# Reordering the first attention steps and the first block of a fused attention, gated MLP and top-2 expert kernel

## The chip, the cores and the metric

One core of one Trainium2 chip runs the whole program. The metric is the device time of one execution in microseconds (us). Engines carry the names of the profile: PE is TensorE, DVE is VectorE, ACT is ScalarE, POOL is GpSimd, SP is SyncE, whose queue issues nearly all of the plain loads.

## The reference

Three parts follow one another: attention inside chunks of 64 positions, a gated MLP in float32 precision, and a mixture of 8 experts of which every token uses two.

```python
q, k, v: (4, 8, 576, 64)                       # batch, heads, positions, width of a head
scores = matmul(q_c, k_c.T) / sqrt(64)         # in chunks of 64 positions
attn = exp(scores - max); attn /= sum + 1e-9
x = matmul(attn, v_c)                          # 2304 tokens x 512
h = x @ w_in                                   # 512 x 2048
x = (h * clip(h + 3, 0, 6) / 6) @ w_out        # 2048 x 512
# then: noisy gate, top 2 of 8 experts, w * (relu(x @ w1[e]) @ w2[e]), summed
```

## The kernel before

The 2304 tokens are 18 tiles of 128, in five blocks of 4, 3, 4, 4 and 3 tiles. Each block runs through 16 **units** of the MLP; unit u holds 128 of the 2048 hidden columns. Precision comes from splitting each operand into a high part `hi` and a rest `lo`, and from three products per matmul (hi·hi, hi·lo, lo·hi: `PASSES`). In a unit, `mlp_s1` multiplies the block's tokens by w_in (12 matmuls of 128x512), `mlp_act` makes the activation g (ACT writes r at L329, DVE finishes r at L330, ACT writes g's hi part at L331), `mlp_lo` (DVE, L336) makes g's lo part, and `mlp_o` adds g times w_out to four accumulators (12 matmuls). PE works one unit ahead: `mlp_o` of unit u comes after `mlp_s1` of unit u+1.

In block 0 the weights aren't there yet in that form. They arrive as 32 **halves** of 512 KB in a 64-bit format: half 2u is w_in of unit u, half 2u+1 its w_out. Each half is turned into hi and lo by five steps: a shift (DVE, L162), the sign bits (DVE, L163), the low bits (DVE, L171), the hi part (ACT, `conv_hi`, L178) and the lo part (DVE, `conv_lo`, L185). The first two are `conv_1`, the third is `conv_2`, and each of the three DVE steps before the hi part reads what the one ahead of it wrote. Block 0 converts in unit u the halves b = 2u+3 and a = 2u+4. When the low bits of half s are done, half s+7 (for s < 10) or s+3 (for s >= 14) is loaded into the raw buffer that came free (`load64`, L150).

Attention of block 0's tiles 0 to 3 stands ahead of block 0, written out by hand, with the first conversions and with matmuls on a constant (`keep_warm`, L679) between. Attention of block 1's three tiles runs inside block 0, four units for each, as pieces k = 0 to 3: scores and row maximum and half of the exponentials (k = 0), the others, the sum's reciprocal and half of the scaling (k = 1), the rest of the scaling (k = 2), transposes and the product with v (k = 3). The functions `att_sc`, `att_mx`, `att_e`, `att_r`, `att_n`, `att_ns`, `att_pt`, `att_at`, `att_xo`, `att_hi`, `att_lo` are these pieces. PE's pieces are put between matmuls by `tick`.

On PE, DVE and ACT the order of the program is the order in which the Python code calls these functions (`manual_schedule`), and each engine works off its own list in that order, one instruction waiting for its inputs while all behind it wait too. SP's list is in program order as well.

Of the kernel before, what the change touches and what calls it, by code (L numbers as in the profile page):

```python
# [19 lines left out]
P = 128  # L20
# [32 lines left out]
def tile_kernel(ctx, tc, qkv, w1u, w2u, wg, noise, out):  # L53
# [89 lines left out]
    def load64(s):  # L143
        if 0 <= s < 2 * U1:
            if s in (3, 4, 5, 6, 10, 11, 12, 13):
                i = (s - 3) % 7
                raw = rawx[i // 2][:, (i % 2) * 2 * DM:(i % 2 + 1) * 2 * DM]
            else:
                raw = work.tile([P, 2 * DM], I32, tag="raw", bufs=3, name="raw")
            nc.sync.dma_start(raw, w1u[s // 2, s % 2])  # L150
            st["raw64", s] = raw

    def conv_1(s):
        if s >= 2 * U1:
            return
        j, h = divmod(s, 2)
        if h == 0:
            st["w", "m", j] = wpool.tile([P, 2, 2 * DM], F32R, tag="w", bufs=U1, name="w")
        raw = st["raw64", s].rearrange("p (n c) -> p n c", c=2)
        hi32 = raw[:, :, 1]  # L160
        u = work.tile([P, DM], I32, tag="x2", bufs=3, name="u")
        nc.vector.tensor_scalar(u, hi32, 3, 0x3fffffff, op0=ALU.logical_shift_left, op1=ALU.bitwise_and)  # L162
        nc.vector.scalar_tensor_tensor(u, hi32, -0x40000000, u, op0=ALU.bitwise_and, op1=ALU.bitwise_or)  # L163
        st["u", s] = u

    def conv_2(s):
# [5 lines left out]
        load64(s + 7 if s < 10 else s + 3 if s >= 14 else -1)  # L172

    def conv_hi(s):
        if s >= 2 * U1:
# [14 lines left out]
    def att_sc(t, pair=0):  # L190
        qt, kt, vt = st["qkv", t]
        sc = middle(pair).rearrange("p (r h k) -> p r h k", r=2, h=KD)
        for hp in range(KD):
            for c in range(2):
                for r in range(2):
                    s = slice(r * 64, r * 64 + 64)
                    nc.tensor.matmul(sc[c * 64:c * 64 + 64, r, hp, :], qt[s, hp, c, :], kt[s, c, hp, :],  # L197
                                     start=True, stop=True)
        st["sc", t] = sc
# [22 lines left out]
        else:  # L222
            nc.scalar.activation(sm, sm, AF.Exp, scale=0.125)

    def att_r(t):
# [3 lines left out]
        nc.vector.tensor_scalar(su, su, 1e-9, None, op0=ALU.add)  # L229
        nc.vector.reciprocal(su, su)  # L230

    def att_n(t):
        att_r(t)
        sm, su, mx, acts = st["att", t]
        nc.vector.tensor_tensor(sm, sm, su.to_broadcast([P, 8, 64]), op=ALU.mult)

    def att_ns(t, heads):
        sm, su, mx, acts = st["att", t]
# [11 lines left out]
    def att_at(t, at):  # L250
        nc.scalar.activation(at.rearrange("p k n -> p (k n)"), st.pop(("pt", t)), AF.Copy)
        st["attT", t] = at

    def att_xo(t, pair=0):
# [35 lines left out]
    def s1(dst, w, x, t0, n):  # L290
        k = 0
        for kd in range(KD):
            for a, b in PASSES:
                nc.tensor.matmul(dst, w[:, a, kd * P:(kd + 1) * P], x[:, b, kd, t0:t0 + n],  # L294
                                 start=(k == 0), stop=(k == 3 * KD - 1))
                k += 1
                if k % 4 == 0:
                    tick()

    def s2(acc, g, w, tiles, first, last):  # L300
        for i in range(tiles):
            gi = tile_of(g, i)
            for j, (a, b) in enumerate(PASSES):
                nc.tensor.matmul(acc[i][:gi.shape[2]], gi[:, a], w[:, b, DM:],  # L304
                                 start=(first and j == 0), stop=(last and j == 2))
            tick()
# [12 lines left out]
    def mlp_s1(b, u, g, off):  # L319
        n = BT[b] * P  # L320
        h = hbank(n)
        s1(h, st["w", "m", u], xb[b], 0, n)
        st["h", b] = h
        st["g", b, u] = g[:, off:off + 2 * n].rearrange("p (j n) -> p j n", j=2)

    def mlp_act(b, u):
# [4 lines left out]
        nc.scalar.activation(st["g", b, u][:, 0], r, AF.Copy)  # L331
        st["r", b] = r

    def mlp_lo(b, u):
        g = st["g", b, u]
# [409 lines left out]
    with tc.manual_schedule(engines={nc.tensor.engine, nc.vector.engine, nc.scalar.engine}):  # L745
        att_sc(0, 0), att_mx(0, False), att_e(0), att_n(0)
        keep_warm(7)
        att_sc(1, 1), att_pt(0, 0), att_at(0, at_[0])
        att_mx(1, True), att_e(1)
        att_sc(2, 2), att_mx(2, True)  # L750
        att_sc(3, 3), att_mx(3, False)
        att_xo(0, 0), att_hi(0), att_e(3), att_e(2)
        keep_warm(3)
        att_n(1), att_pt(1, 1), att_at(1, at_[1])
        keep_warm(5)
        att_lo(0), conv_1(0)
        att_n(3), att_pt(3, 3), att_xo(1, 1), att_hi(1), att_at(3, at_[0])
        att_n(2), att_pt(2, 2), att_at(2, at_[1])
        conv_2(0), conv_hi(0)
        att_lo(1)  # L760
        att_xo(3, 3), att_hi(3), att_xo(2, 2), att_hi(2)
        conv_lo(0), att_lo(3), att_lo(2)
# [98 lines left out]

    def block0():
        nonlocal prev
        n0 = st.get("tick", 0)
        for i in range(BT[1]):
            k = n0 + 28 * i
            t = LT + i
            at(ticks, k + 3, att_sc, t)
            at(ticks, k + 3 * 7 - 4 + 3, att_pt, t)
            at(ticks, k + 3 * 7 + 3, att_xo, t)  # L870
        for u in range(U1):

            t, k = LT + u // 4, (u % 4 if u < 4 * BT[1] else None)
# [11 lines left out]
            b, a = 2 * u + 3, 2 * u + 4  # L885
            conv_1(b)
            mlp_lo(0, u)
            conv_2(b)
            conv_hi(b)
            if k == 0:  # L890
                att_mx(t, True)
                att_e(t, range(4))
            elif k == 1:
                att_r(t)
                att_ns(t, range(4))
            elif k == 3:
                att_hi(t)
# [196 lines left out]
```

## Time and profile before

| | before |
|---|---|
| three runs, us | 935.14, 935.76, 937.75 (median 935.76) |
| the profiled execution, us | 934.58 |
| its span in the profile, us | 932.8 |
| PE / DVE / ACT busy over the span | 98% / 52% / 36% |
| PE's granted clock over the span | 0.998 of full |

The shares are averages over a span of which the part at issue is about an eighth: block 0 and the attention ahead of it end near 126 us, and there DVE is the busy engine.

### The profile page before, as it was taken

To read this page: it belongs to the slowest core of one execution; us is meant where nothing else is said; L and a number is where in the kernel's file an instruction comes from. 1 tells how busy PE (TensorE), PEld (TensorE's weight loads), DVE (VectorE), ACT (ScalarE), POOL (GpSimd) and SP (SyncE) were. 2 spreads that over 40 slices of the span, in tenths; PEclk is the share of its full clock that TensorE was granted. 3 is DMA by queue.
4 is the path that set the end of the run, shared out by engine and by line. 5 is a ranking of instruction groups with operands and counts; after the bars stand their busy time and mean duration, and the time that the engine had idled before them with its cause. 6 is when DMAs were issued, how large, how long until landed. Compare 5 with 4: busy or idle time off the path is not lost.

```text
span 932.8 us, 14436 instructions
## 1 busy us (share of the span) xinstructions
PE 913.1 (98%) x5814; PEld 766.3 (82%) x5814; DVE 482.2 (52%) x912; ACT 333.2 (36%) x643; POOL 231.9 (25%) x213
## 2 busy tenths in 40 slices
PE   6999999999999999999999999999999999999996
PEld 3677788887777777788988898898988889888885
DVE  6999965454454443537543555444545454441311
ACT  5565433333233322344541443333434333321210
POOL 0000000030002000033203345754645445332321
PEclk9999999999999999999999999999999999999999
DMA  9636639113112410024541764653746355240422
GB/s 342 204 112 193 193 98 372 61 37 101 35 34 58 136 35 1 1 69 113 156 139 15 191 145 116 151 121 113 145 117 128 111 128 127 69 54 20 54 25 33
DMA packets 49916, 101.49 MB, mean 109 GB/s; under 512 B 17040, under 2 KB 23056, under 8 KB 49840
## 3 DMA queue, kind: packets, MB, share of 16 engines
q1 hardware_dynamic: 38736, 80.38, 27.4%
q0 software_dynamic: 11104, 20.10, 11.9%
q8 instruction: 47, 0.77, 0.4%
q14 instruction: 29, 0.24, 0.1%
HBM read 77.66 MB, written 22.75 MB: 108 GB/s over the span
## 4 chain that ended last, share of the span: by engine, by line
PE 86%; DVE 10%; ACT 2%; issue 1%; DMA 0%; POOL 0%; POOLq 0%; DVEq 0%; ACTq 0%
PE bp L304 41%; PE bp L294 40%; DVE u L171 2%; DVE u L163 2%; DVE u L162 1%; DVE r L330 1%; DVE w L185 1%; DVE g L336 1%; PE pair L197 1%; PE pair L264 1%; PE pair L247 1%; ACT w L178 1%; PE bp L581 0%; ACT r L329 0%; DMA xr<-x2d,tab 0%
## 5 line engine op out<-in xcount | busy, mean ns | idle before, releaser
L304 PE MATMUL bp<-w,g 128*128 128x512 f32 (+1 forms) x1812 | 453.9, 396 | 0.4 <-ACT g L331 0.3
L304 PEld LDWEIGHTS bp<-w,g 128*128 128x128 f32 (+1 forms) x1812 | 328.3, 185 | 73.7 <-DVE g L336 0.8
L294 PE MATMUL bp<-Xa,w 128*128 128x304 f32 (+3 forms) x1344 | 244.2, 332 | 2.3 <-ACT w L178 1.9
L294 PEld LDWEIGHTS bp<-Xa,w 128*128 128x128 f32 x1344 | 209.0, 188 | 30.4 <-ACT w L178 5.2
L554 POOL DMA_INDIRECT xrq<-x2d,iq x114 | 119.5, 1048 | 95.7 <-DVE iq L548 34.4
L597 DVE SCALAR_TENSOR_TENSOR g<-bp,g 128x304 fp32r<-128x304 f32 (+2 forms) x128 | 60.4, 472 | 130.9 <-ACT g L596 130.9
L139 DVE TENSOR_TENSOR w<-raw,w 128x1024 fp32r<-128x1024 f32 x64 | 78.4, 1226 | 89.0 <-ACT w L138 89.0
L519 POOL DMA_INDIRECT table<-pay,slot x36 | 36.3, 1009 | 338.9 <-DVE slot L516 247.9
L596 ACT ACTIVATE g<-bp 128x304 fp32r<-128x304 f32 (+2 forms) x128 | 54.3, 424 | 168.6 <-PE bp L294 168.5
L294 PE MATMUL bp<-Xb,w 128*128 128x384 f32 (+1 forms) x480 | 106.1, 366 | 0.0
L294 PE MATMUL bp<-Xe,w 128*128 128x304 f32 (+1 forms) x672 | 102.7, 308 | 0.0
L294 PEld LDWEIGHTS bp<-Xe,w 128*128 128x128 f32 x672 | 99.8, 188 | 3.3
L330 DVE SCALAR_TENSOR_TENSOR r<-r,bp 128x512 f32<-128x512 f32 (+1 forms) x80 | 50.6, 632 | 91.8 <-ACT r L329 91.6
L294 PEld LDWEIGHTS bp<-Xb,w 128*128 128x128 f32 x480 | 85.3, 188 | 12.5 <-issue 1.8
L624 POOL DMA_INDIRECT out_dram<-arena,tab x40 | 62.7, 1567 | 123.5 <-DVE arena L621 100.1
L329 ACT ACTIVATE r<-bp,b 128x512 f32<-128x512 f32 (+1 forms) x80 | 51.3, 642 | 106.4 <-PE bp L294 106.4
L138 ACT ACTIVATE w<-raw 128x1024 fp32r<-128x1024 f32 x64 | 67.7, 1058 | 58.8 <-PE bp L304 58.5
L336 DVE TENSOR_TENSOR g<-r,g 128x512 fp32r<-128x512 f32 (+1 forms) x80 | 51.0, 637 | 40.2 <-ACT g L331 40.2
L331 ACT ACTIVATE g<-r 128x512 fp32r<-128x512 f32 (+1 forms) x80 | 47.2, 590 | 60.3 <-DVE r L330 60.3
L178 ACT ACTIVATE w<-u 128x512 fp32r<-128x512 f32 x32 | 20.3, 633 | 32.5 <-DVE u L171 32.5
L372 DVE STREAM_TRANSPOSE arena<-xrq 128x512 f32<-128x512 f32 (+1 forms) x30 | 31.4, 1046 | 0.1
L735 POOL MEMSET zero<- 128x1024 f32 x1 | 1.0, 952 | 115.1 <-DVE u L171 115.1
(148 smaller groups left out, 483.8 us busy)
## 6 DMA issues: line engine op xcount, KB each, us to landing
raw<-in_w2u_dram SPq DMA_DIRECT2D x64, 512.0 KB, 4.0
raw<-in_w1u_dram SPq DMA_DIRECT2D x24, 512.0 KB, 4.9
arena<-in_qkv_dram SPq DMA_DIRECT2D x14, 768.0 KB, 4.1
out_dram<-zero SPq DMA_DIRECT2D x4, 1536.0 KB, 19.4
rawx<-in_w1u_dram SPq DMA_DIRECT2D x8, 512.0 KB, 8.4
x2d<-x SPq DMA_DIRECT2D x15, 256.0 KB, 3.4
xq<-x2d SPq DMA_DIRECT2D x44, 64.0 KB, 3.4
xrq<-x2d,iq POOLq DMA_INDIRECT x114, 2.6
```

The costliest lines, as they stand in the source:

```text
L138: nc.scalar.activation(w[:, 0], raw, AF.Copy)
L139: nc.vector.tensor_tensor(w[:, 1], raw, w[:, 0].bitcast(F32), op=ALU.subtract)
L294: nc.tensor.matmul(dst, w[:, a, kd * P:(kd + 1) * P], x[:, b, kd, t0:t0 + n], start=(k == 0), stop=(k == 3 * KD - 1))
L304: nc.tensor.matmul(acc[i][:gi.shape[2]], gi[:, a], w[:, b, DM:], start=(first and j == 0), stop=(last and j == 2))
L329: nc.scalar.activation(r, st["h", b], AF.Relu, bias=b3)
L330: nc.vector.scalar_tensor_tensor(r, r, 6.0, st["h", b], op0=ALU.min, op1=ALU.mult)
L331: nc.scalar.activation(st["g", b, u][:, 0], r, AF.Copy)
L336: nc.vector.tensor_tensor(g[:, 1], st["r", b], g[:, 0].bitcast(F32), op=ALU.subtract)
L554: nc.gpsimd.indirect_dma_start(out=xr[:, c * P:(c + 1) * P], out_offset=None, in_=x2q, in_offset=bass.IndirectOffsetOnAxis(ap=st["iq", key ...
L596: nc.scalar.activation(g[:, 0, t0:t0 + n], h, AF.Relu)
L597: nc.vector.scalar_tensor_tensor(g[:, 1, t0:t0 + n], h, 0.0, g[:, 0, t0:t0 + n].bitcast(F32), op0=ALU.max, op1=ALU.subtract)
L624: s = nc.gpsimd.indirect_dma_start(out=out, out_offset=bass.IndirectOffsetOnAxis(ap=tab[:n, i, 0:1], axis=0), in_=y, in_offset=None, compu ...
```

## The change

It changes the order of the steps ahead of block 0 and in block 0, and nothing behind.

- The conversion is cut into `conv_1`, `conv_2`, `conv_3`, and the load that follows it is a call of its own, `load_next`.
- Ahead of block 0: halves 0 and 2 (w_in of units 0 and 1) are converted, of half 1 only two steps; tile 1's scaling goes to POOL, tile 0's copy of the transposes to DVE; the tiles use other PSUM pairs; 18 constant matmuls instead of 28; tiles 4 and 5 are loaded between the halves.
- In block 0: half a comes ahead of half b, the steps of both are interleaved with others, half b's lo part is made in the next unit (`late`), and attention starts two units later (`lag`).
- `mlp_s1` and `mlp_o` of block 0 take all of one product, then all of the next.

```diff
+    def load_next(*halves):
+        for s in halves:
+            load64(s + 7 if s < 10 else s + 3 if s >= 14 else -1)
...
+        passes = None
+        if b == 0:
+            passes = ((0, 0), (1, 0), (0, 1)) if u == 0 else ((0, 0), (0, 1), (1, 0))
+        s1(h, st["w", "m", u], xb[b], 0, n, passes)
...
-        att_sc(1, 1), att_pt(0, 0), att_at(0, at_[0])
+        att_sc(1, 3), att_pt(0, 0)
         att_mx(1, True), att_e(1)
...
-        keep_warm(6)
-        conv_1(1), conv_2(1), conv_hi(1)
-        conv_1(2), conv_2(2), conv_hi(2)
-        conv_lo(1), conv_lo(2)
+        att_at(0, at_[0], True)
+        att_sc(2, 1), att_mx(2, False), att_e(2)
+        att_sc(3, 2), att_mx(3, True), att_e(3)
+        att_xo(0, 0)
+        keep_warm(4, "p2")
+        att_r(1), att_nm(1, nc.gpsimd)
+        att_n(2), conv_1(0)
+        att_pt(1, 3), att_at(1, at_[1])
+        att_pt(2, 1), att_at(2, at_[0])
+        att_xo(1, 3), att_hi(0)
+        att_n(3), att_pt(3, 2)
+        conv_2(0), conv_3(0)
+        att_at(3, at_[1]), att_hi(1)
+        att_xo(2, 1), att_xo(3, 2)
+        conv_hi(0), att_hi(2), att_hi(3)
+        att_lo(0), att_lo(1), conv_lo(0), att_lo(2), att_lo(3)
+        conv_1(2), conv_2(2), conv_3(2), conv_hi(2)
+        conv_1(1), conv_2(1)
+        load_next(0)
...
             mlp_s1(0, u, gtile(), 0)
+            mlp_r(0, u)
             if k == 3:
                 att_at(t, at_[0])
-            mlp_act(0, u)
+            mlp_g(0, u)
+            if u == 0:
+                conv_3(1), conv_hi(1), conv_lo(2)
+                load_next(1, 2)
+                late = [1]
+            else:
+                conv_lo(*late)
...
-            conv_1(b)
-            mlp_lo(0, u)
-            conv_2(b)
-            conv_hi(b)
+            conv_1(a), conv_2(a)
+            mlp_lo(0, u)
+            if u == 0:
+                conv_lo(*late)
+            conv_1(b)
+            conv_3(a), conv_hi(a)
+            conv_2(b)
             if k == 0:
                 att_mx(t, True)
+            elif k == 1:
+                att_r(t)
+            elif k == 3:
+                att_hi(t)
+            conv_3(b), conv_hi(b)
+            conv_lo(a)
+            if k == 0:
                 att_e(t, range(4))
             elif k == 1:
-                att_r(t)
                 att_ns(t, range(4))
...
-            conv_1(a)
-            conv_2(a)
-            conv_hi(a)
-            conv_lo(b)
-            if k == 3:
-                att_lo(t)
-            conv_lo(a)
+            late = [b]
+            load_next(b, a)
```

DVE, block 0, from the finishing of r in one unit to the same step in the next, in a unit without attention on DVE. `u` with a number is the half being converted, `w` its split form, `r` and `g` the activation. Before (unit 2; L171 is the low bits, L185 the lo part):

```order
L330 SCALAR_TENSOR_TENSOR r_558<-r_558,bp4_428 128x512
L162 TENSOR_SCALAR u_578<-raw_354 128x512
L163 SCALAR_TENSOR_TENSOR u_578<-raw_354,u_578 128x512
L336 TENSOR_TENSOR g_545<-r_558,g_545 128x512
L171 SCALAR_TENSOR_TENSOR u_578<-raw_354,u_578 128x512
L162 TENSOR_SCALAR u_587<-raw_405 128x512
L163 SCALAR_TENSOR_TENSOR u_587<-raw_405,u_587 128x512
L171 SCALAR_TENSOR_TENSOR u_587<-raw_405,u_587 128x512
L185 TENSOR_TENSOR w_536<-u_578,w_536 128x512
L185 TENSOR_TENSOR w_586<-u_587,w_586 128x512
L330 SCALAR_TENSOR_TENSOR r_614<-r_614,bp3_427 128x512
```

And now (unit 1; the same steps are L352, L160, L167, L364, L174, L191):

```order
L352 SCALAR_TENSOR_TENSOR r_468<-r_468,bp3_411 128x512
L191 TENSOR_TENSOR w_391<-u_445,w_391 128x512
L160 TENSOR_SCALAR u_486<-rawx_120 128x512
L167 SCALAR_TENSOR_TENSOR u_486<-rawx_120,u_486 128x512
L364 TENSOR_TENSOR g_455<-r_468,g_455 128x512
L160 TENSOR_SCALAR u_490<-rawx_120 128x512
L174 SCALAR_TENSOR_TENSOR u_486<-rawx_120,u_486 128x512
L167 SCALAR_TENSOR_TENSOR u_490<-rawx_120,u_490 128x512
L174 SCALAR_TENSOR_TENSOR u_490<-rawx_120,u_490 128x512
L191 TENSOR_TENSOR w_485<-u_486,w_485 128x512
L352 SCALAR_TENSOR_TENSOR r_513<-r_513,bp4_412 128x512
```

Between the last low-bits step and the next r two lo parts stood before; now one stands there, and the other has moved behind r.

ACT, block 0, the unit that starts a tile's attention (k = 0), up to the next unit's r and g. Rows with `w<-u` are hi parts, rows with `mx` and x4 are four exponentials. Before (unit 0 and the start of unit 1):

```order
L329 ACTIVATE r_462<-bp4_428,b3_81 128x512
L331 ACTIVATE g_433<-r_462 128x512
L178 ACTIVATE w_408<-u_466 128x512
L220 ACTIVATE arena_94,su_475<-pair0_72,mx_473 128x64 x4
L178 ACTIVATE w_481<-u_482 128x512
L329 ACTIVATE r_503<-bp3_427,b3_81 128x512
```

And now (unit 2 and the start of unit 3):

```order
L351 ACTIVATE r_513<-bp4_412,b3_81 128x512
L356 ACTIVATE g_500<-r_513 128x512
L184 ACTIVATE w_546<-u_547 128x512
L184 ACTIVATE w_485<-u_551 128x512
L226 ACTIVATE arena_94,su_558<-pair0_72,mx_556 128x64 x4
L351 ACTIVATE r_584<-bp3_411,b3_81 128x512
```

The exponentials stood between the two hi parts and stand now between the second hi part and the next unit's r.

## Rows read from the trace of the kernel before

**Rows 1.** Busy time by stretch: us, then each engine's busy us, granted PE clock, DMA share, GB/s.

```profile
10.00:20.00 10.00, 6.36 (x150) 4.17 (x148) 8.45 (x21) 7.64 (x38) 0.00 (x0) 1.00 1.03 408
24.26:123.92 99.66, 97.27 (x576) 72.56 (x577) 94.50 (x169) 54.80 (x141) 0.95 (x1) 1.00 0.51 160
```

**Rows 2.** Timeline of DVE, unit 12 of block 0: start us, us, engine, line.

```profile
106.47 0.68 DVE L330 SCALAR_TENSOR_TENSOR r<-r,bp 128x512 f32<-128x512 f32 x1
...
107.52 0.69 DVE L163 SCALAR_TENSOR_TENSOR u<-raw,u 128x512 int32<-128x512 int32 x1
...
109.34 0.42 DVE L162 TENSOR_SCALAR u<-raw 128x512 int32<-128x512 int32 x1
109.79 0.69 DVE L163 SCALAR_TENSOR_TENSOR u<-raw,u 128x512 int32<-128x512 int32 x1
110.52 0.69 DVE L171 SCALAR_TENSOR_TENSOR u<-raw,u 128x512 int32<-128x512 int32 x1
111.13 1.47 DVE L185 TENSOR_TENSOR w<-u,w 128x512 fp32r<-128x512 f32 x2
112.52 0.68 DVE L330 SCALAR_TENSOR_TENSOR r<-r,bp 128x512 f32<-128x512 f32 x1
```

**Rows 3.** Timeline of ACT beside the end of that unit.

```profile
111.24 0.63 ACT L178 ACTIVATE w<-u 128x512 fp32r<-128x512 f32 x1 [1.16 <-DVE u L171]
111.78 0.67 ACT L329 ACTIVATE r<-bp,b 128x512 f32<-128x512 f32 x1
113.23 0.63 ACT L331 ACTIVATE g<-r 128x512 fp32r<-128x512 f32 x1 [0.78 <-DVE r L330]
```

**Rows 4.** Timeline of ACT, units 0 and 1: exponentials (first and fourth) and scalings.

```profile
31.94 0.32 ACT L220 ACTIVATE arena<-pair,mx 128x64 f32<-128x64 f32 x1 [0.23 <-DVE mx L209]
...
32.83 0.32 ACT L220 ACTIVATE arena<-pair,mx 128x64 f32<-128x64 f32 x1
...
38.45 1.05 ACT L240 ACTIVATE arena<-arena,su 128x64 f32<-128x64 f32 x4
```

**Rows 5.** Timeline of DVE, unit 0: the row maximum and its scaling.

```profile
30.96 0.68 DVE L205 TENSOR_REDUCE mx<-pair 128x8 f32<-128x512 f32 x1
31.68 0.17 DVE L209 TENSOR_SCALAR mx<-mx 128x8 f32<-128x8 f32 x1
```

**Rows 6.** DMA issues of the page: count, KB each, median us to landing.

```profile
raw<-in_w2u_dram SPq DMA_DIRECT2D x64, 512.0 KB, 4.0
raw<-in_w1u_dram SPq DMA_DIRECT2D x24, 512.0 KB, 4.9
```

**Rows 7.** Timeline, units 6 and 7: half 18 is issued, half 18 is used.

```profile
70.35 2.12 SPq L150 DMA_DIRECT2D raw<-in_w1u_dram  x2
...
76.75 0.42 DVE L162 TENSOR_SCALAR u<-raw 128x512 int32<-128x512 int32 x1
```

**Rows 8.** Timeline of the steps ahead of block 0 and of its first r.

```profile
10.06 0.17 DVE L209 TENSOR_SCALAR mx<-mx 128x8 f32<-128x8 f32 x1
...
22.66 1.46 PE L679 MATMUL pair<-ones 128*128 128x512 bf16 x6 [1.15 <-DVE Xa L277]
...
24.26 2.99 PE L294 MATMUL bp<-Xa,w 128*128 128x512 f32 x12
...
28.09 0.68 DVE L330 SCALAR_TENSOR_TENSOR r<-r,bp 128x512 f32<-128x512 f32 x1
```

**Rows 9.** A POOL group of the page: busy, mean ns of one, idle before.

```profile
L735 POOL MEMSET zero<- 128x1024 f32 x1 | 1.0, 952 | 115.1 <-DVE u L171 115.1
```

**Rows 10.** Timeline of PE at the end of block 0.

```profile
121.12 2.96 PE L304 MATMUL bp<-w,g 128*128 128x512 f32 x12
123.92 2.25 PE L294 MATMUL bp<-Xb,w 128*128 128x384 f32 x12
126.01 2.94 PE L304 MATMUL bp<-w,g 128*128 128x512 f32 x12
```

More of the change, by code (lines that the diff above doesn't have):

```diff
@@ L155, in conv_1, with conv_2, conv_3 @@
             return
[L156 to L161, printed above, removed]
-        nc.vector.tensor_scalar(u, hi32, 3, 0x3fffffff, op0=ALU.logical_shift_left, op1=ALU.bitwise_and)
+        if s % 2 == 0:
+            st["w", "m", s // 2] = wpool.tile([P, 2, 2 * DM], F32R, tag="w", bufs=U1, name="w")
+        hi32 = st["raw64", s].rearrange("p (n c) -> p n c", c=2)[:, :, 1]
+        u = st["u", s] = work.tile([P, DM], I32, tag="x2", bufs=3, name="u")
+        nc.vector.tensor_scalar(u, hi32, 3, 0x3fffffff, op0=ALU.logical_shift_left, op1=ALU.bitwise_and)
+    def conv_2(s):
+        if s >= 2 * U1:
+            return
+        hi32 = st["raw64", s].rearrange("p (n c) -> p n c", c=2)[:, :, 1]
+        u = st["u", s]
         nc.vector.scalar_tensor_tensor(u, hi32, -0x40000000, u, op0=ALU.bitwise_and, op1=ALU.bitwise_or)
-        st["u", s] = u
-    def conv_2(s):
+    def conv_3(s):
         if s >= 2 * U1:
@@ L171, in conv_2 @@
         nc.vector.scalar_tensor_tensor(u, lo32, 29, u, op0=ALU.logical_shift_right, op1=ALU.bitwise_or)
-        load64(s + 7 if s < 10 else s + 3 if s >= 14 else -1)
+    def load_next(*halves):
+        for s in halves:
+            load64(s + 7 if s < 10 else s + 3 if s >= 14 else -1)
     def conv_hi(s):
@@ L223, in att_e, with att_r @@
             nc.scalar.activation(sm, sm, AF.Exp, scale=0.125)
-    def att_r(t):
+    def att_r(t, eng=None):
+        eng = eng or nc.vector
         sm, su, mx, acts = st["att", t]
@@ L228, in att_r, with att_nm @@
             nc.vector.tensor_reduce(su, sm, axis=AX.X, op=ALU.add)
-        nc.vector.tensor_scalar(su, su, 1e-9, None, op0=ALU.add)
+        eng.tensor_scalar(su, su, 1e-9, None, op0=ALU.add)
         nc.vector.reciprocal(su, su)
+    def att_nm(t, eng=None):
+        sm, su, mx, acts = st["att", t]
+        (eng or nc.vector).tensor_tensor(sm, sm, su.to_broadcast([P, 8, 64]), op=ALU.mult)
     def att_n(t):
         att_r(t)
-        sm, su, mx, acts = st["att", t]
-        nc.vector.tensor_tensor(sm, sm, su.to_broadcast([P, 8, 64]), op=ALU.mult)
+        att_nm(t)
     def att_ns(t, heads):
@@ L248, in att_pt, with att_at @@
         st["pt", t] = pt
-    def att_at(t, at):
-        nc.scalar.activation(at.rearrange("p k n -> p (k n)"), st.pop(("pt", t)), AF.Copy)
+    def att_at(t, at, dve=False):
+        dst, src = at.rearrange("p k n -> p (k n)"), st.pop(("pt", t))
+        if dve:
+            nc.vector.tensor_copy(dst, src)
+        else:
+            nc.scalar.activation(dst, src, AF.Copy)
         st["attT", t] = at
@@ L288, in tile_kernel, with s1, s2 @@
     PASSES = ((0, 0), (0, 1), (1, 0))
[L290 to L301, printed above, removed]
+    def s1(dst, w, x, t0, n, passes=None):
+        if passes:
+            todo = [(kd, a, b) for a, b in passes for kd in range(KD)]
+        else:
+            todo = [(kd, a, b) for kd in range(KD) for a, b in PASSES]
+        for k, (kd, a, b) in enumerate(todo):
+            nc.tensor.matmul(dst, w[:, a, kd * P:(kd + 1) * P], x[:, b, kd, t0:t0 + n],
+                             start=(k == 0), stop=(k == 3 * KD - 1))
+            if k % 4 == 3:
+                tick()
+    def s2(acc, g, w, tiles, first, last, passes=None):
+        if passes:
+            todo = [(i, j, a, b) for j, (a, b) in enumerate(passes) for i in range(tiles)]
+        else:
+            todo = [(i, j, a, b) for i in range(tiles) for j, (a, b) in enumerate(PASSES)]
+        for k, (i, j, a, b) in enumerate(todo):
             gi = tile_of(g, i)
[L303 to L306, printed above, removed]
+            nc.tensor.matmul(acc[i][:gi.shape[2]], gi[:, a], w[:, b, DM:],
+                             start=(first and j == 0), stop=(last and j == 2))
+            if k % 3 == 2:
+                tick()
     ACC = ["p0", "p1", "p2", "p5", "p6"]
@@ L321, in mlp_s1, with mlp_r @@
         h = hbank(n)
-        s1(h, st["w", "m", u], xb[b], 0, n)
+        passes = None
+        if b == 0:
+            passes = ((0, 0), (1, 0), (0, 1)) if u == 0 else ((0, 0), (0, 1), (1, 0))
+        s1(h, st["w", "m", u], xb[b], 0, n, passes)
         st["h", b] = h
         st["g", b, u] = g[:, off:off + 2 * n].rearrange("p (j n) -> p j n", j=2)
-    def mlp_act(b, u):
+    def mlp_r(b, u):
         n = BT[b] * P
@@ L330, in mlp_act, with mlp_g @@
         nc.vector.scalar_tensor_tensor(r, r, 6.0, st["h", b], op0=ALU.min, op1=ALU.mult)
-        nc.scalar.activation(st["g", b, u][:, 0], r, AF.Copy)
         st["r", b] = r
+    def mlp_g(b, u):
+        nc.scalar.activation(st["g", b, u][:, 0], st["r", b], AF.Copy)
+    def mlp_act(b, u):
+        mlp_r(b, u)
+        mlp_g(b, u)
     def mlp_lo(b, u):
@@ L340, in mlp_o @@
             st["acc", b] = [bank(ACC[i], [P, DM], "acc") for i in range(BT[b])]
-        s2(st["acc", b], st.pop(("g", b, u)), st["w", "m", u], BT[b], u == 0, u == U1 - 1)
+        s2(st["acc", b], st.pop(("g", b, u)), st["w", "m", u], BT[b], u == 0, u == U1 - 1,
+           PASSES[::2] + PASSES[1:2] if b == 0 else None)
     def x2_out(b):
@@ L673, in tile_kernel, with keep_warm @@
     nc.scalar.preload_act_table_set("natural_log_exp_and_others")
-    warm = bank("p4", [P, 4, P], "warm")
-    def keep_warm(n):
+    def keep_warm(n, tag="p4"):
+        warm = bank(tag, [P, 4, P], "warm")
         for i in range(n):
@@ L697, in tile_kernel @@
     load_part(3, bufs[3], 2, 3)
-    for i in range(1, 7):
+    for i in range(1, 3):
         load64(i)
+    load_tile(BT[0], bufs[BT[0]])
+    for i in range(3, 7):
+        load64(i)
+    load_tile(BT[0] + 1, bufs[BT[0] + 1])
     def constants():
@@ L747, in tile_kernel @@
         keep_warm(7)
-        att_sc(1, 1), att_pt(0, 0), att_at(0, at_[0])
+        att_sc(1, 3), att_pt(0, 0)
         att_mx(1, True), att_e(1)
[L750 to L762, printed above, removed]
-        keep_warm(6)
-        conv_1(1), conv_2(1), conv_hi(1)
-        conv_1(2), conv_2(2), conv_hi(2)
-        conv_lo(1), conv_lo(2)
+        att_at(0, at_[0], True)
[17 more added lines that the diff above has]
+        load_next(0)
     first.__exit__(None, None, None)
@@ L769, in tile_kernel @@
     single.update((tag, halves.tile([P, DM], F32, name="b" + tag)) for tag, (i, j) in in_pair.items() if i)
-    for t in (LT, LT + 1):
-        load_tile(t, bufs[t])
     def at(d, u, f, *a):
@@ L863, in block0 @@
         nonlocal prev
-        n0 = st.get("tick", 0)
+        n0, lag = st.get("tick", 0), 2
         for i in range(BT[1]):
-            k = n0 + 28 * i
+            k = n0 + 7 * (4 * i + lag)
             t = LT + i
             at(ticks, k + 3, att_sc, t)
-            at(ticks, k + 3 * 7 - 4 + 3, att_pt, t)
-            at(ticks, k + 3 * 7 + 3, att_xo, t)
+            at(ticks, k + 20, att_pt, t)
+            at(ticks, k + 24, att_xo, t)
+        late = []
         for u in range(U1):
-            t, k = LT + u // 4, (u % 4 if u < 4 * BT[1] else None)
+            t, k = LT + (u - lag) // 4, ((u - lag) % 4 if lag <= u < lag + 4 * BT[1] else None)
+            b, a = 2 * u + 3, 2 * u + 4
             mlp_s1(0, u, gtile(), 0)
+            mlp_r(0, u)
             if k == 3:
                 att_at(t, at_[0])
-            mlp_act(0, u)
+            mlp_g(0, u)
[3 more added lines that the diff above has]
+                late = [1]
+            else:
+                conv_lo(*late)
             for pb, v in prev:
@@ L884, in block0 @@
                 att_ns(t, range(4, 8))
-            b, a = 2 * u + 3, 2 * u + 4
+            conv_1(a), conv_2(a)
+            mlp_lo(0, u)
+            if u == 0:
+                conv_lo(*late)
             conv_1(b)
-            mlp_lo(0, u)
+            conv_3(a), conv_hi(a)
             conv_2(b)
-            conv_hi(b)
             if k == 0:
                 att_mx(t, True)
+            elif k == 1:
[5 more added lines that the diff above has]
+            if k == 0:
                 att_e(t, range(4))
             elif k == 1:
-                att_r(t)
                 att_ns(t, range(4))
             elif k == 3:
-                att_hi(t)
+                att_lo(t)
                 if t + 2 < NTILE:
                     load_tile(t + 2, bufs[4 + t % 2])
-            conv_1(a)
-            conv_2(a)
-            conv_hi(a)
-            conv_lo(b)
-            if k == 3:
-                att_lo(t)
-            conv_lo(a)
+            late = [b]
+            load_next(b, a)
     nxt = {"u": U1}
```

## The prediction

> **What bounds the kernel now.** I read the table of busy time by stretch first. Between the first matmul of block 0 and the first of block 1 lie 99.66 us, 16 units, in which DVE is busy for 94.5 us [rows 1]. PE's 97.27 us there contain waits inside its matmuls, so its figure is no measure. What PE needs is shown where nothing holds it: 12 matmuls of 128x512 take 2.80 us (121.12 to 123.92) [rows 10], so a unit with 24 of them wants 5.6 us, below the 6.05 us that a unit takes (106.47 to 112.52) [rows 2].
>
> The timelines of DVE and ACT, laid side by side, tell what the 6.05 us are. Call R the start of DVE's r step and T the start of the last low-bits step of the unit (110.52). From R to T is 4.05 us of DVE work. From T to the next R are 2.00 us, and this is a chain over two engines: T at 110.52, ACT's hi part at 111.24 (0.72 later), ACT's r at 111.78 (0.54), DVE's r at 112.52 (0.74) [rows 2, 3]. ACT works off its list in order, so r of the next unit cannot pass the hi part, although its matmuls are done. DVE spends these 2.00 us on two lo parts, 1.39 us from the first to the end of the pair, and so it looks busy: the chain is hidden behind work that happens to be as long.
>
> The prices on DVE come from the same unit. A 128x512 step whose follower does not need its result gives way after 0.61 us (107.52 to 109.34 is three of them); if the follower needs it, after 0.73 (109.79 to 110.52); the shift gives way after 0.45 to a dependent step (109.34 to 109.79) [rows 2]. A shift with an independent follower is not in the trace. I take its length less the overlap of the others, 0.42 - 0.08 = 0.34; between 0.30 and 0.45 the sum moves by under 2 us over the block.
>
> **The change, part by part.**
>
> First, the steps ahead of block 0. Up to 10.06 us nothing that matters moves [rows 8]. Tile 0's copy leaves ACT, so ACT's first eight exponentials start 0.26 us behind the scaled maximum, at 10.32. Four take 1.19 us (0.89 us from the first to the fourth, and a third of that more) [rows 4], eight 2.38; then tile 2's single exponential, 0.54; then tile 3's eight, to 15.6. DVE's sum correction, reciprocal and scaling of tile 3 (some 0.2, 0.2 and 0.7 us) end at 16.9, PE's transposes at 17.6. Behind them stand in ACT's list tile 3's copy and four hi parts, at 0.54 us each [rows 3], ending at 20.4. Block 0's first matmul no longer waits for the six constant matmuls that took it from 22.66 to 24.26 [rows 8], and starts at 20.4. DVE makes tile 3's lo part at 20.5 and three conversion steps of half 2; their T is 22.3, and 2.00 us later is the first R: 24.3 in place of 28.09 [rows 8], **3.8 us earlier**. Of this the POOL scaling is the unknown. The only POOL row of any size writes 1024 elements in 0.95 us [rows 9], 0.48 for 512. Two reads and a write at that rate are 1.43 us, which I take: issued at 13.5 it ends at 14.9, and tile 1's transposes end as ACT's exponentials do. Its ends are 0.48, which changes nothing, and twice 1.43, which with tile 2's scaling held up behind it would cost 1.6 us. If ACT never waited for tile 3's transposes, 0.5 us would be gained: the gain lies between 2.2 and 4.3. The Trainium skill (GPSIMD Engine Reference, section Performance versus the Vector engine) has 4497 ns for 2048 elements, by which this would be an estimated 1.1 us and the sum the same. The other loads of this stretch have slack: half 3 is wanted at 28 us.
>
> Second, the chain in a unit. Now the path from R to T holds five independent steps (r, the late lo part, a's sign bits, g's lo part, a's low bits: 3.04), a's shift (0.45), b's shift (0.34) and b's sign bits, whose follower still needs them (0.73): 4.56 us in place of 4.05. From T on nothing is shorter: b's hi part, r on ACT, r on DVE, 2.00 us. Only one lo part (0.61) is left to do in them. So DVE's work falls from 6.05 to 5.77, but a unit takes **6.56 us**: the saved dependence is spent on an idle 0.8 us in front of r.
>
> Third, attention on that chain. In k = 0 the maximum and its scaling (0.72 and 0.17) [rows 5] come between b's two last steps, which takes their dependence away: R to T is 5.33. The four exponentials now stand in ACT's list between b's hi part and r: 1.19 more, so 8.52 us, where the unit at 28.09 had taken 6.84. In k = 1 the two small steps (0.34) make it 4.78, and four scalings, 1.05 less an overlap of 0.09 [rows 4], stand in front of r: 7.74. In k = 2 and 3 it is 6.56 (the copy of the transposes is hidden now, behind DVE's r). A tile takes 29.38 us.
>
> The sum from the first R: unit 0 has two more DVE steps, 7.78; unit 1 6.56; three tiles 88.1; unit 14, with one half and g's lo part behind g, 5.21 (1.42, 0.61, 0.45, 0.73 and 2.00); and from the last R to the matmuls of g, 1.42 (0.72 from r to ACT's g, as from 112.52 to 113.23 [rows 2, 3], its 0.63 and a gap). That is 109.1 us. Before, from 28.09 to the matmuls at 126.01 [rows 8, 10], it was 97.92. **Longer by 11.2 us.** PE has cover in all of it: it needs 5.6 us of every 6.56.
>
> Fourth, the loads. From half 18 on, half s+3 takes the buffer of half s. Half a of unit u is issued when b of unit u-1 has its low bits. Before, b was the first half of a unit and a the second of the next: half 18 issued at 70.35, used at 76.75, 6.4 us [rows 7]. Now b is last and a is first: from T plus 0.72 to the next R plus 1.21, which is 2.5 us in a bare unit, 3.7 behind k = 0 and 3.4 behind k = 1. A half lands 4.0 us after its issue by the median of the many later loads of this size, 4.9 by that of these loads, some of which queue at the start [rows 6]. I take 4.0 and 0.05 for the wake-up. DVE's list stands still meanwhile, g's lo part too. Units 7 to 13 pay: three of them follow a bare unit (1.56 each), two k = 0 (0.37), two k = 1 (0.60): **6.6 us**; at 3.5 us of landing 3.4, at 4.9 it is 12.9.
>
> The late loads of tiles 6 to 8, the product-wise order of PE's matmuls and the moved constants I cost at nothing: PE has a whole unit in hand, and the same matmuls run. If that cover is gone, it shows as PE waits.
>
> Sum: -3.8 + 11.2 + 6.6 = **14.0 us**. The profiled execution took 934.58, the median of the runs is 1.18 above; by the median the change takes 935.76 + 14.0 = **949.8**.
>
> **One rule against the trace.** The trace has 0.61 and 0.73 us for the same step with an independent and a dependent follower [rows 2]. The Trainium skill (VectorE: DVE Perf Modes, section The DRAIN you can't avoid) says that the next step waits for the pipe in any case and that a semaphore between costs nothing extra; by it, taking dependent steps apart brings nothing. The row speaks against it. As a mechanism of this kernel: the apart-taken pairs (one shift in 15 units, one sign step in six) would cost the dependent price after all, 0.12 each, 21 times, 2.5 us more: 952.3.
>
> **The rivals.**
> - *DVE's own work sets the unit, and the change pays.* The place is the step from T to the next R. If r on ACT did not stand behind b's hi part, units would take 5.77 and tiles 24.7; with 7.0 for unit 0, 5.8 for unit 1 and 6.3 at the end, bound there by PE, the block has 93.0 from first R to last g, 4.9 less than before, and with 3.8 ahead of it the time would be 927.1. For it: DVE's 94.5 of 99.66. Against it: the 2.00 us fit to 0.01 in every bare unit that I read. It decides if the path from T to R is under 1.2 us.
> - *The loads land in time.* Then 6.6 falls away: 943.2. For it: isolated loads may be quicker than the median. It decides at 2.5 us of landing.
> - *Slow loads.* At 4.9 us of landing: 956.1.
> - *It comes out even.* If exponentials and scalings cost the chain nothing (6.5 less) and the loads land in time, 936.7, within 0.3%.
> - *PE's clock falls* in the longer gaps. It was granted full speed in a stretch with PE busy for 6.36 of 10 us [rows 1]; the new units have 5.6 of 6.6 to 8.5. Each 24 matmuls at the lower level would cost 5.6 us, of which most of the gap pays.
>
> **How the numbers follow.** Chances: my forecast, loads at 3.5 to 4.6 us, 0.55; loads in time 0.15; slow loads or a fallen clock 0.10; the rule 0.05; even 0.05; DVE's own work 0.10. A measurement of this kernel tells 0.3% (2.8 us) from no change. So slower 0.85, the same 0.05, faster 0.10. The range takes in the ends of my sum and the case of loads in time with a good first stretch, and leaves out the two cases that are not slower: 941 to 957.
>
> **What would show it.** Right: the first r of DVE near 24.3; then r to r 6.56 in bare units, 8.5 and 7.7 in k = 0 and 1; DVE idle in front of r, released by ACT's r, in each unit; DVE's shift released by a DMA in units 7 to 13; block 1's first matmul near 137 instead of 123.92; nothing changed behind. Wrong: DVE above 95% busy in block 0, or bare units under 6.05.

## The result, and the profile after

| | before | after |
|---|---|---|
| median, us (5 runs each) | 935.29 (934.45 to 937.75) | 943.96 (942.90 to 945.02) |
| ratio after / before | | 1.009, 95% interval 1.0073 to 1.0107 |
| the profiled execution / its span, us | 934.58 / 932.8 | 942.9 / 941.1 |

The change makes the kernel 8.7 us slower. Direction and range held; the size did not, 14.0 us forecast.

I read the same stretch in both traces, from the first r of block 0 to the fifteenth. Busy time by stretch, the kernel before (us, then PE, PEld, DVE, ACT, POOL busy with instruction counts, granted PE clock, DMA share, GB/s):

```profile
28.09:118.57 90.48, 88.09 (x510) 65.33 (x509) 86.67 (x156) 50.73 (x134) 0.95 (x1) 1.00 0.52 162
```

and the changed kernel:

```profile
24.09:125.72 101.63, 88.62 (x538) 66.71 (x537) 86.12 (x157) 50.95 (x135) 0.95 (x1) 0.98 0.50 158
```

DVE does no more than before, 86.1 us against 86.7, but the same 14 units take 11.15 us longer: 15.5 us of DVE's stretch are idle, where 3.8 were. What the idle time waits for stands in the waits of DVE (engine, line, what was waited for: us in total, times, longest), after, from 25 to 126 us:

```profile
DVE r L352 <- ACT r L351: 13.8, 11, 1.9
DVE u L160 <- DMA raw<-in_w1u_dram: 0.5, 1, 0.5
```

and before, from 28 to 119 us, the one line of this view:

```profile
DVE r L330 <- ACT r L329: 1.1, 3, 0.4
```

So nearly all of the new idle time stands in front of r, as forecast, and hardly any behind a load. It stands in 11 of the 14 units; in the three of k = 3 DVE makes a lo part of the attention tile in that time and has no wait. One bare unit after, on DVE (it answers to [rows 2]):

```profile
31.80 0.69 DVE L352 SCALAR_TENSOR_TENSOR r<-r,bp 128x512 f32<-128x512 f32 x1 [0.68 <-ACT r L351]
32.41 0.68 DVE L191 TENSOR_TENSOR w<-u,w 128x512 fp32r<-128x512 f32 x1
...
34.67 0.42 DVE L160 TENSOR_SCALAR u<-rawx 128x512 int32<-128x512 int32 x1
35.01 0.69 DVE L174 SCALAR_TENSOR_TENSOR u<-rawx,u 128x512 int32<-128x512 int32 x1
35.61 0.69 DVE L167 SCALAR_TENSOR_TENSOR u<-rawx,u 128x512 int32<-128x512 int32 x1
36.33 0.69 DVE L174 SCALAR_TENSOR_TENSOR u<-rawx,u 128x512 int32<-128x512 int32 x1
36.94 0.68 DVE L191 TENSOR_TENSOR w<-u,w 128x512 fp32r<-128x512 f32 x1
38.30 0.69 DVE L352 SCALAR_TENSOR_TENSOR r<-r,bp 128x512 f32<-128x512 f32 x1 [0.67 <-ACT r L351]
```

and on ACT (it answers to [rows 3]):

```profile
37.06 0.63 ACT L184 ACTIVATE w<-u 128x512 fp32r<-128x512 f32 x1 [0.70 <-DVE u L174]
37.59 0.67 ACT L351 ACTIVATE r<-bp,b 128x512 f32<-128x512 f32 x1
```

From r at 31.80 to b's low bits at 36.33 are 4.53 us, from there over ACT (37.06, 37.59) to the next r at 38.30 are 1.97. DVE has one lo part (36.94) to fill those 1.97 us, and then stands for 0.67.

The ends of the block, on PE, answer to [rows 8, 10]:

```profile
20.05 3.02 PE L310 MATMUL bp<-Xa,w 128*128 128x512 f32 x12 [1.28 <-ACT Xa L288]
...
131.54 2.25 PE L310 MATMUL bp<-Xb,w 128*128 128x384 f32 x12
133.63 1.55 PE L322 MATMUL bp<-w,g 128*128 128x512 f32 x6
```

The accounts of the two profiled executions: the first r falls at 24.09 instead of 28.09 (-4.00), from there to the last g matmuls are 109.54 us instead of 97.92 (+11.62), and 0.70 comes behind block 0. Together 8.32, the difference of their times. The 0.70 is no effect that can be told: from the last g matmuls of block 0 to the end of the span the eleven profiled executions of this document, of all its kernels, take between 806.0 and 807.9 us.

### The profile page after: what moved, and what is told of

It reads as the page before. It is cut to its first block, busy times and chain, and to the rows that moved or that the text cites. A ratio compares the mean times of both kernels' runs of the same rounds, so it can differ in the third digit from the quotient of the medians.

```text
span 941.1 us, 14415 instructions
## 1 busy us (share of the span) xinstructions
PE 910.5 (97%) x5804; PEld 766.3 (81%) x5804; DVE 480.6 (51%) x912; ACT 332.4 (35%) x642; POOL 231.8 (25%) x214
## 5 line engine op out<-in xcount | busy, mean ns | idle before, releaser
L310 PE MATMUL bp<-Xa,w 128*128 128x304 f32 (+3 forms) x1344 | 241.2, 330 | 2.1 <-ACT Xa L288 1.3
L352 DVE SCALAR_TENSOR_TENSOR r<-r,bp 128x512 f32<-128x512 f32 (+1 forms) x80 | 50.7, 634 | 105.7 <-ACT r L351 105.3
L364 DVE TENSOR_TENSOR g<-r,g 128x512 fp32r<-128x512 f32 (+1 forms) x80 | 50.9, 637 | 39.7 <-ACT g L356 39.5
```

What stands on the lines that cost most here:

```text
L364: nc.vector.tensor_tensor(g[:, 1], st["r", b], g[:, 0].bitcast(F32), op=ALU.subtract)
```

## The experiments

Two theories stood against each other. A: the path from r to b's last step and on over ACT sets a unit. B: DVE's own work does, or PE's. All runs are compared with the kernel before on the same chip; its median there lay between 934.0 and 934.3. Beside the changed kernel it had been 935.29. The times expected below start mostly from the changed kernel's 943.96, so they can be met no closer than some 1.3 us; r to r, read from the traces, is the sharper measure.

### The attention pieces ahead of b's hi part in ACT's list

```diff
             if k == 0:
                 att_mx(t, True)
+                att_e(t, range(4))
             elif k == 1:
                 att_r(t)
+                att_ns(t, range(4))
...
             conv_3(b), conv_hi(b)
             conv_lo(a)
-            if k == 0:
-                att_e(t, range(4))
-            elif k == 1:
-                att_ns(t, range(4))
```

> Edit: in block 0, ACT's first four exponentials (k = 0) and first four scalings (k = 1) of an attention tile stand in ACT's list ahead of half b's hi part instead of behind it. Theory A, the chain over ACT (b's hi part, attention pieces, r) sets the unit: the pieces now begin about when DVE starts b's last step, so they hide 0.66 us (exponentials) and 0.58 us (scalings) of themselves behind it; six such units, 3.7 us less than the changed kernel: 940.2 us. Intervals of DVE's r: k = 0 7.7 instead of 8.36, k = 1 7.0 instead of 7.60, bare units 6.50 as they are. Theory B, DVE's own work or PE sets the unit: nothing changes, 944.0.

Measured: 940.44 us, ratio 1.0065 (1.0051 to 1.0079). r to r is 7.84 in k = 0 (8.35 in the changed kernel), 7.10 in k = 1 (7.60) and 6.50 in bare units. A unit of k = 0 on DVE, from one r to the next:

```profile
39.26 0.69 DVE L352 SCALAR_TENSOR_TENSOR r<-r,bp 128x512 f32<-128x512 f32 x1 [0.67 <-ACT r L351]
...
47.10 0.69 DVE L352 SCALAR_TENSOR_TENSOR r<-r,bp 128x512 f32<-128x512 f32 x1 [1.34 <-ACT r L351]
```

DVE's and PE's work is the same, only the place of eight small instructions in ACT's list is another, so B falls for these units. The gain is smaller than expected: five of the six units give 0.5 us each, and the third unit of k = 0 gives none, since there DVE now waits 1.2 us for a load (0.5 in the changed kernel). From the first r to the last g matmuls that is 2.4 us less, where 3.7 were expected; that the time met 940.2 is in part luck.

### A lo part moved onto the path

```diff
-            conv_3(b), conv_hi(b)
             conv_lo(a)
+            conv_3(b), conv_hi(b)
```

> Edit: in each unit of block 0 DVE makes half a's lo part ahead of half b's last step instead of behind it; the work is the same and no step waits for the one ahead of it. Theory A, the path from r to b's last step and on over ACT sets the unit: that path gets 0.61 us longer and loses one dependence of 0.12: bare units 6.99 instead of 6.50, k = 0 and k = 1 0.61 more, 8 us over the block: 952 us. Theory B, DVE's own work sets the unit: one dependence less in nine units, 0.12 each: 943 us.

Measured: 952.45 us, ratio 1.0191 (1.0175 to 1.0206). A bare unit takes 7.16, 0.17 above what A gave: a's lo part now comes so soon that it waits for a's hi part on ACT. DVE and then ACT in one of them:

```profile
120.15 0.69 DVE L352 SCALAR_TENSOR_TENSOR r<-r,bp 128x512 f32<-128x512 f32 x1 [2.23 <-ACT r L351]
...
123.96 0.68 DVE L167 SCALAR_TENSOR_TENSOR u<-raw,u 128x512 int32<-128x512 int32 x1
124.74 0.69 DVE L191 TENSOR_TENSOR w<-u,w 128x512 fp32r<-128x512 f32 x1
...
127.31 0.69 DVE L352 SCALAR_TENSOR_TENSOR r<-r,bp 128x512 f32<-128x512 f32 x1 [1.27 <-ACT r L351]
```

```profile
124.08 0.63 ACT L184 ACTIVATE w<-u 128x512 fp32r<-128x512 f32 x1 [1.62 <-DVE u L174]
```

The lo part starts 0.78 us behind the sign bits (123.96 to 124.74) instead of 0.61, when a's hi part is done. B said 943 and is out. The same ten steps of DVE in another order cost 8 to 9 us.

### The new first steps with the old units

The units of block 0 as the kernel before has them; ahead of block 0 this is added:

```diff
         conv_1(1), conv_2(1)
-        load_next(0)
+        conv_3(1), conv_hi(1)
+        conv_lo(2), conv_lo(1)
+        load_next(0, 1, 2)
```

> Edit: the new first steps and the product-wise order of the matmuls stay; block 0's units are written in the old order again (half b whole, then half a whole, both lo parts last, attention from unit 0, each load behind its half). Theory A, the order in the unit alone makes the loss: half 1 is again converted ahead of the first r, so the first r falls near 26.0 (24.09 in the changed kernel, 28.09 before), then intervals as before (6.05 bare, 97.9 from the first r to the last g matmuls): 933.2 us, faster than both kernels, ratio 0.998. Theory C, the loss comes with the product-wise matmul order or the earlier tile loads: block 0 stays near 109 us and the time at 943 to 945.

Measured: 933.15 us (11 runs), ratio 0.999 (0.9981 to 0.9999). The first r falls at 26.35, and all units after it are within 0.05 us of those before. So the loss sits in the order of the units alone; the product-wise order of the matmuls and the earlier tile loads cost nothing. It also prices the first steps: of the 4.0 us by which r comes earlier in the changed kernel some 2 are half 1's last steps, which were put off into unit 0 (over the kernels with the same first steps the first r fell between 24.09 and 25.24, so this is good to a microsecond).

### The two loads of a unit the other way round

```diff
-            load_next(b, a)
+            load_next(a, b)
```

> Edit: the two loads at the end of a unit are issued in the other order, so that the first half of the next unit but one (type a) takes the buffer that half b has just left, and the second (type b) that of half a. Theory A, this is the buffer on which the forecast's loads term rested, and its price was right for that case: stalls of DVE's shift of 1.5 to 1.9 us in bare units and 0.4 to 1.0 behind attention pieces, in seven units: 6 to 9 us more than the changed kernel, 950 to 953 us. Theory D, a lone load lands in about 2.5 us and the term is zero in either order: 944 us, no wait of DVE for a load over 0.5 us.

Measured: 950.90 us, ratio 1.0175 (1.016 to 1.0191). The waits of DVE from the first r to block 1:

```profile
DVE r L352 <- ACT r L351: 15.3, 13, 1.9
DVE u L160 <- DMA raw<-in_w1u_dram: 8.7, 7, 2.1
```

Seven waits, together 8.7 us, in the seven units that I had named, where 6.6 were forecast. The price was about right, for a buffer that the changed kernel does not use. In the changed kernel the timelines of DVE and of SP's queue show it: a half's load goes out as soon as half a, not half b, has its low bits.

```profile
92.89 0.69 DVE L174 SCALAR_TENSOR_TENSOR u<-raw,u 128x512 int32<-128x512 int32 x1
94.21 0.69 DVE L174 SCALAR_TENSOR_TENSOR u<-raw,u 128x512 int32<-128x512 int32 x1
...
97.98 0.43 DVE L160 TENSOR_SCALAR u<-raw 128x512 int32<-128x512 int32 x1 [0.51 <-DMA raw<-in_w1u_dram]
```

```profile
93.60 0.33 SPq L150 DMA_DIRECT2D raw<-in_w1u_dram  x1
```

Issued at 93.60, before b's last step (94.21) is even done, and landed at 97.98, 4.38 us later. That is the only wait for a load in the block. The twelve loads issued between 60 and 110 us landed in 3.7 to 4.5 us, with a median of 4.1, close to the 4.0 that I took.

### r ahead of b's hi part

If the path over ACT is the cause, the cure is to let r pass b's hi part. PE has the matmuls of r done a unit ahead, so this needs only another order of the calls. `mlp_r` is cut in two for it, ACT's step and, as `mlp_rv`, DVE's.

```diff
-            mlp_s1(0, u, gtile(), 0)
-            mlp_r(0, u)
+            if u == 0:
+                mlp_s1(0, u, gtile(), 0)
+                mlp_r(0, u)
+            mlp_rv(0, u)
...
             conv_3(a), conv_hi(a)
+            if u + 1 < U1:
+                mlp_s1(0, u + 1, gtile(), 0)
+                mlp_r(0, u + 1)
             conv_2(b)
```

> Edit: in block 0 the first matmuls of unit u + 1 and ACT's r of unit u + 1 are written behind half a's hi part of unit u, so that r stands in ACT's list ahead of half b's hi part; DVE's and PE's own orders do not change. Theory A, r waiting in ACT's list behind b's hi part is what sets the unit: without it DVE's work does, 5.8 us in bare units, 6.6, 6.0, 5.8 and 6.4 in k = 0 to 3, some 93.5 us from the first r to the last g matmuls (109.5 in the changed kernel): 928 us, if the loads keep up. But half a's load then has only 3.2 to 4.0 us until it is wanted and lands in 3.8 to 4.4: waits of about 0.6 us in seven units: 932 us. Rival P, PE has no time to spare either (24 matmuls 5.6 us and attention pieces): units of 6.05 on the average, 931.5 us, with DVE waiting for g or ACT for PE and not for a DMA. Rival B, the order in ACT's list does not matter: 944 us.

Measured: 929.81 us, ratio 0.9945 (0.9931 to 0.9959). r to r is 5.74 in bare units, and the waits of DVE from 25 to 120 us are turned round:

```profile
DVE u L160 <- DMA raw<-in_w1u_dram: 2.4, 5, 1.0
DVE r L355 <- ACT r L351: 0.2, 1, 0.2
```

A holds, B falls, and as forecast the loads come next, less than expected (2.4 us for 4). They can be given more time with buffers that are there already:

```diff
-            if s in (3, 4, 5, 6, 10, 11, 12, 13):
+            if s % 7 > 2 and s < 28:
...
-            load64(s + 7 if s < 10 else s + 3 if s >= 14 else -1)
+            load64(s + 7 if s < 24 else 31 if s == 28 else -1)
```

> Edit: the same, and the halves go round over all seven buffers to the end (the four that lie in weight slots are used for halves 17 to 20 and 24 to 27 too), so that each half is loaded three units ahead instead of one. Theory A: the waits for the loads fall away, 928 us, the first r to the last g matmuls 93.5 us, faster than both kernels. Rival P, PE: the same 931.5 us as without the buffers.

Measured: 927.48 us, ratio 0.9921 (0.9908 to 0.9935), the fastest of all, 6.8 us below the kernel before on the same chip. Busy time by stretch, first to fifteenth r:

```profile
24.42:110.18 85.76, 84.28 (x537) 65.85 (x536) 84.80 (x157) 50.07 (x135) 0.95 (x1) 1.00 0.58 184
```

DVE is busy for 84.8 of 85.8 us. The work is that of the changed kernel (86.1); the 15.5 idle us are down to 1. So the rival that PE has no time to spare, 931.5 us with the buffers or without, falls too. A unit on DVE, in which no step waits:

```profile
98.12 0.68 DVE L355 SCALAR_TENSOR_TENSOR r<-r,bp 128x512 f32<-128x512 f32 x1
98.72 0.68 DVE L191 TENSOR_TENSOR w<-u,w 128x512 fp32r<-128x512 f32 x1
...
102.64 0.69 DVE L174 SCALAR_TENSOR_TENSOR u<-rawx,u 128x512 int32<-128x512 int32 x1
103.25 0.68 DVE L191 TENSOR_TENSOR w<-u,w 128x512 fp32r<-128x512 f32 x1
103.85 0.68 DVE L355 SCALAR_TENSOR_TENSOR r<-r,bp 128x512 f32<-128x512 f32 x1
```

on ACT, r (102.57) now stands ahead of b's hi part (103.36):

```profile
102.04 0.63 ACT L184 ACTIVATE w<-u 128x512 fp32r<-128x512 f32 x1 [1.33 <-DVE u L174]
102.57 0.67 ACT L351 ACTIVATE r<-bp,b 128x512 f32<-128x512 f32 x1
103.36 0.63 ACT L184 ACTIVATE w<-u 128x512 fp32r<-128x512 f32 x1
```

The buffers by themselves, on the changed kernel:

> Edit: the changed kernel with nothing but the seven buffers to the end. Theory A: only its one wait of DVE for a load in block 0 (0.5 us) falls away, since 6.5 us units leave each load enough time: 943.5 us. Rival, the loads hold up the changed kernel in ways that its waits do not show: the 2.3 us that the buffers gave with r ahead, 941.6 us.

Measured: 942.80 us, ratio 1.0094 (1.0078 to 1.0109); the wait of 0.51 us is gone and no other. 942.8 lies between the two expectations and its interval does not part them; the intervals of r do (6.49 to 6.50 bare, 8.35 and 7.60 as without the buffers), so the loads hold up nothing else.

### r ahead of a's hi part in the kernel before

```diff
             conv_1(a)
             conv_2(a)
+            if u + 1 < U1:
+                mlp_s1(0, u + 1, gtile(), 0)
+                mlp_r(0, u + 1)
             conv_hi(a)
```

> Edit, on the kernel before and not on the changed one: in block 0 the first matmuls and ACT's r of unit u + 1 are written ahead of half a's hi part of unit u. All else is the kernel before. Theory A: there DVE has two lo parts to do while the chain over ACT runs (1.39 of its 2.00 us), and the second of them needs a's hi part, which now comes behind r; so a bare unit falls only from 6.05 to some 5.95, the others by 0.1 to 0.2, 2 us over the block: 932.3 us. The gain of the two kernels with r ahead needs the new order of DVE's steps as well. Rival: r's place in ACT's list is worth the same 6.5 us by itself: 928 us.

Measured: 932.77 us (11 runs), ratio 0.9993 (0.9984 to 1.0002): no difference that can be told in the time. Bare units did not fall by 0.1 but stayed at 6.05. Only the three units of k = 2 got shorter, 6.05 for 6.50: there the copy of the transposes had stood on ACT between a's hi part and r, and r now passes it. From the first r to the last g matmuls the trace has 96.69 us for 97.92. DVE and then ACT in a bare unit:

```profile
109.22 0.69 DVE L171 SCALAR_TENSOR_TENSOR u<-raw,u 128x512 int32<-128x512 int32 x1
109.83 1.47 DVE L185 TENSOR_TENSOR w<-u,w 128x512 fp32r<-128x512 f32 x2
111.22 0.68 DVE L335 SCALAR_TENSOR_TENSOR r<-r,bp 128x512 f32<-128x512 f32 x1
```

```profile
108.69 0.67 ACT L329 ACTIVATE r<-bp,b 128x512 f32<-128x512 f32 x1
109.94 0.63 ACT L178 ACTIVATE w<-u 128x512 fp32r<-128x512 f32 x1 [0.58 <-DVE u L171]
```

ACT's r is long done (108.69), but the second lo part needs a's hi part, which starts at 109.94, when a's low bits are done. The pair of lo parts takes the same 1.39 us, and the next r comes 2.00 us after the last low bits as ever. So in a bare unit of the kernel before two paths over ACT end together, one through r and one through the last lo part; the prediction saw the first and took the lo parts for work that happens to be as long. The changed kernel had moved the last lo part off, which is what makes r's place worth 0.76 us in a bare unit (6.50 to 5.74).

### Tile 1's scaling back on DVE

```diff
-        att_r(1), att_nm(1, nc.gpsimd)
+        att_r(1), att_nm(1)
```

> Edit: tile 1's scaling goes back from GpSimd to DVE. It takes some 0.7 us there instead of 1.04, starts at 13.3 and ends at 14.0 instead of 14.25, and moves DVE's scaling of tile 2 back by 0.7, less the 0.4 us that a small DVE step took longer beside GpSimd. Theory A, the first matmul of block 0 hangs on tile 3's attention (ACT's exponentials and copies): it moves by under 0.3 us (20.05 in the changed kernel, and up to a us of spread between executions in where the first r falls). Rival, the scalings on DVE are on the path: 0.4 to 0.7 us later.

Measured, one execution: 942.48 us, first matmul of block 0 at 20.33 (20.05 with GpSimd), first r at 24.37 (24.09). No more than the spread between executions; this one shows no effect of the scaling's place.

## Why the prediction was right in direction and wrong in size

- **First steps, -3.8.** Right: -4.00 in the profile (up to 1.2 less in other executions of the same steps), the first matmul at 20.05 (20.4 forecast), released by ACT's hi part of tile 3's x as worked out. POOL's scaling takes 1.04 us (taken 1.43, ends 0.48 and 2.86).
- **The chain in a unit, +11.2.** Right: bare units 6.50 (6.56), k = 0 8.35 (8.52), k = 1 7.60 (7.74), unit 0 7.71 (7.78), unit 14 5.15 (5.21). Without the 0.51 us for the load, first r to last g matmuls is 109.03 us; 109.1 was forecast. That this sum fits so closely is luck: two errors of some 1.3 us cancel in it. The three tiles take 86.9 us without the wait for the load, not 88.1, and from the last r to the last g matmuls are 2.76 us, not 1.42, since block 1's first matmuls (131.54, for 2.09 us) stand ahead of those on PE. The experiments moved single pieces of this path both ways, and r to r moved with them: by -0.5 us where 0.6 to 0.7 were expected, and by +0.66 for 0.49. The last r of the block on DVE, to be read beside PE's lines above:

```profile
130.87 0.69 DVE L352 SCALAR_TENSOR_TENSOR r<-r,bp 128x512 f32<-128x512 f32 x1 [1.27 <-ACT r L351]
```
- **The loads, +6.6.** This step failed: 0.5 us. The prediction says "Half a of unit u is issued when b of unit u-1 has its low bits". Of the two calls in `load_next(b, a)` the first loads the next half of type a, since s + 3 turns odd into even, and it gets the buffer that came free first, half a's. So half a is issued some 1.3 us earlier than I took it, and a landing of 4.38 us costs half a microsecond once. The other loads of type a landed in time. With the calls swapped the stalls are there, 8.7 us in seven places, and the time is 950.9. The mechanism was sound and its price near (6.6 for 8.7); the buffer was wrong. Without the term my sum is 943.2, the case "the loads land in time", which I gave 0.15. It happened, by another way than the quicker landing that I named for it.
- **The rule drawn from the Trainium skill** (VectorE: DVE Perf Modes, section The DRAIN you can't avoid), that taking dependent steps apart brings nothing. The same section adds that a next op that is not held starts earlier, which the prediction left out. The trace stays against the rule and agrees with the addition, since an independent follower starts 0.60 us into a step of 0.69 (35.01 to 35.61): the shift with an independent follower gives way after 0.34 us (34.67 to 35.01), with a dependent one after 0.45 as in [rows 2], and the sign bits after 0.72 where b's low bits need them (35.61 to 36.33). The rival built on it, 952.3, fell: with it a bare unit would have taken 6.68 us (6.56 and 0.12), and 6.50 were measured.
- **DVE's own work sets the unit, 927.1.** The condition was named, r not standing behind b's hi part. It doesn't hold in the changed kernel. Where an experiment made it hold, with the loads in time, bare units took 5.73 to 5.74 us (5.77 forecast), a tile 24.4 (24.7), and first r to last g matmuls 94.04 (93.0). The time was 927.48; that it lies so near to 927.1 is in part luck, as the kernel before was 1.5 us faster on that chip than the 935.76 from which I reckoned.
- **PE's clock.** It did fall once, and cost nothing. PE's groups around it in the changed kernel:

```profile
43.28 2.88 PE L310 MATMUL bp<-Xa,w 128*128 128x512 f32 x12
48.05 4.64 PE L322 MATMUL bp<-w,g 128*128 128x512 f32 x12 [1.89 <-ACT g L356]
52.53 2.90 PE L310 MATMUL bp<-Xa,w 128*128 128x512 f32 x12
```

Busy time by stretch, the same place:

```profile
44.00:48.00 4.00, 2.17 (x10) 1.47 (x8) 2.15 (x5) 3.02 (x12) 0.00 (x0) 1.00 0.70 226
48.00:52.00 4.00, 3.95 (x10) 2.92 (x11) 3.93 (x10) 1.81 (x9) 0.00 (x0) 0.57 0.00 1
```

After four microseconds in which PE was busy for 2.17 and waited 1.89 for ACT's g, the granted clock is 0.57 for a stretch of four, near the lower of the two levels (1.2 GHz); twelve matmuls take 4.64 us for 2.9. PE is a unit ahead, and the unit then running takes 7.60 us from r to r, as the other units of its kind at full clock. In the kernel with a's lo part on the path the clock fell in four places (0.58 from 84 to 88 us, for one), and all its bare units still took 7.16.

## What to carry to other kernels

Where two engines pass work to and fro, write down the path from a step of one unit to the same step of the next, over every list that it goes through; taking work or dependences off an engine pays only if that path gets shorter too, and one that waits in a strict list counts all that stands ahead of it. When one wait is taken off such a path, look for a second that ends at the same time: here the new order of DVE's steps alone costs time, and r's place alone is worth 1.2 us in the trace and nothing that can be told in the time; both together, with the new first steps and more buffers for the loads, give 0.8%. For a load that waits for a buffer, follow which buffer it gets; order of calls and parity of the index decided here between one wait of 0.5 us and seven of 8.7 us together.

## What the runs showed of the hardware that was not expected

A small DVE step beside GpSimd's scaling took more than three times as long. In the changed kernel, POOL works from 13.21 to 14.25:

```profile
13.21 1.04 POOL L241 TENSOR_TENSOR lead<-lead,su 128x512 f32<-128x512 f32 x1 [10.95 <-DVE su L237]
13.71 0.57 DVE L236 TENSOR_SCALAR su<-su 128x8 f32<-128x8 f32 x1
```

and with the scaling on DVE the same step is

```profile
14.38 0.17 DVE L236 TENSOR_SCALAR su<-su 128x8 f32<-128x8 f32 x1
```

The row reduction just ahead of it (128x512, 12.99 to 13.68), two thirds of which lie beside POOL's work, kept its 0.69 us. All eight profiled executions with this scaling on GpSimd show the same: the step takes 0.56 to 0.58 us and ends 0.02 to 0.04 us after POOL does, as if it had to let POOL finish. It is one step of the program, and what the two engines share there was not tried.
